# A half-size first gate/up product in the second block, wide score multiplications, and new engine orders

## The chip, the cores and the metric

The kernel runs on one core of one Trainium2 chip. The metric is the device time of one execution in microseconds (us); the time of a kernel is the median of several runs, and one further execution of it is recorded by the hardware profiler. The core has a matrix engine (TensorE; PE in the profile, with PEld for the loading of its weights), a vector engine (VectorE, DVE), an engine for activation functions and copies (ScalarE, ACT), a general engine (GpSimd, POOL) and an engine that only issues transfers here (SyncE, SP). Matrix products are accumulated in eight PSUM banks; everything else on the chip lies in SBUF.

## The reference

One sequence of 2048 tokens of width 1024 is normalised; the result goes through local attention and, beside it, through a gated feed-forward network, and both are joined:

```python
x = A_x
xn = _layernorm(x, axis=-1)
s = _A_ref(xn, A_wqkv, A_wo)           # 32 heads of 32; each token sees itself
...                                    # and the tokens 2, 4, ... 14 before it
g = _silu(_B_ref(xn, B_w1, B_w3, B_w2))  # (silu(xn w1) * (xn w3)) w2, hidden width 3584
return x + s * g
```

The scores of one token are eight products of its query with the keys at distances 0, 2, ..., 14 ("shifts" below), summed over 32 numbers of a head.

## The kernel before

**Tiling.** The tokens are worked in two blocks of 1024 (`b` = 0, 1), each of two chunks of 512 (`c` = 0, 1 and 2, 3). A block does the q, k and v products, the attention of its chunks, the gate and up products of the network in 14 steps (`up_step(b, fb)`, each of 256 hidden columns), and the down and output products.

**Products with fewer multiplications.** Nearly all matrix products are done by a scheme of seven half-size products in place of eight (sums of operand quarters are made on DVE beforehand, and sums of results afterwards on DVE and ACT). In a gate/up step the first of these seven products, `pa` with the weights `w1` and the first half of the normalised tokens, is itself either done plainly (two times four matmuls of 512 columns, named `mm ua` below) or once more by the scheme: `up_first(b, fb)` has seven products of two matmuls of 256 columns each, three copies on ACT (`ufork`, `us5p`, `usnap`) and one add on DVE (`ucc`). `L2F` says for which steps: 1 to 13 in both blocks. `up_first` needs quarter sums of the tokens, made by `x_sums2` (`xt1` to `xt4`), and of the weights, made in block 0 by `w_sums2` (`wss0`, `wss2`, `wss3`), kept in `s2_dram` and loaded in block 1 by the transfer `s2.fb` into the slot of `w1` and `w3`. The larger sums of the weights (`ws0` to `ws3`) go through `s_dram` and come back as `st.fb`.

**Scores.** `scores(c)` goes over the eight shifts `w`. For each it multiplies queries and shifted keys on DVE in two halves of 128x2048 (`qk`), adds the halves (`qa`), and, where two shifts have a pair of buffers, adds on for both shifts at once (`qb`, `qc`) into `E`. The buffers are the three places of the pool `att`.

**What sets the order.** All work is first listed as operations, numbered in the order in which the code makes them. A planner gives each engine a sequence by costs and due times. Then the table `ORDER` (one row each for PE, DVE, ACT, POOL and SP) moves operations: an entry (a, b) puts operation a right behind operation b on its engine. Every engine works strictly in its sequence, and SP and POOL issue transfers in theirs. A slot of the pool `r8` (six buffers of 1 MB) is filled anew only when the work on its old contents is done.

**The second block's start.** The output product `wo(1)` of block 0's second chunk ends while the gate/up steps of block 1 begin. It gathers its result in a slot `o1` of `r8`; products with the gate (`s_g`) and the input (`x_o`) are made on DVE in five pieces, and each piece is stored by a transfer `out` on SP's queue. The slot is then filled with `st.2`, the sums of step 2 of block 1. In the profile the helpers have one line each: L593 and L1283 are the matmuls (plain, and of `up_first`), L602 all two-operand DVE work, L607 ACT copies, L634 all transfers. The tile `a` is the pool `att`, `r` is `r8`, `k` is a pool of f32 halves, `mm` is PSUM.

Of the kernel before, what the change touches and what calls it, by code (L numbers as in the profile page):

```python
# [42 lines left out]
class Plan:  # L43
# [420 lines left out]
def kernel(  # L464
# [17 lines left out]
    CH = 512  # L482
# [7 lines left out]
    NJ = 8  # L490
    NR = 4
# [815 lines left out]
    def w_sums(fb):  # L1307
# [9 lines left out]
        if U2B and fb:  # L1317
            w_sums2(fb)
# [780 lines left out]
```

## Time and profile before

| what | value |
|---|---|
| median of 3 runs | 707.27 us (706.75 to 707.87) |
| the profiled execution's own time | 707.13 us |
| its span, first to last instruction | 705.4 us |
| busy on DVE | 676.4 us, 831 instructions |
| busy on ACT | 385.4 us, 752 instructions |
| busy on POOL | 40.6 us, 83 instructions |
| moved by DMA | 174.06 MB, mean 247 GB/s |

A group row of the profile gives line, engine, operation, output and inputs, shape and count, then busy time, the mean duration of one in ns, and the idle time before. Instructions of one engine overlap: a duration holds the pipeline's end too. So the price of one instruction in a row of them is read from start to start in the timeline, whose rows give start, length, engine and what was done, neighbours of one kind merged.

### The profile page before, as it was taken

To read this page: it belongs to the slowest core of one execution; us is meant where nothing else is said; L and a number is where in the kernel's file an instruction comes from. 1 tells how busy PE (TensorE), PEld (TensorE's weight loads), DVE (VectorE), ACT (ScalarE), POOL (GpSimd) and SP (SyncE) were. 2 spreads that over 40 slices of the span, in tenths; PEclk is the share of its full clock that TensorE was granted. 3 is DMA by queue.
4 is the path that set the end of the run, shared out by engine and by line. 5 is a ranking of instruction groups with operands and counts; after the bars stand their busy time and mean duration, and the time that the engine had idled before them with its cause. 6 is when DMAs were issued, how large, how long until landed. Compare 5 with 4: busy or idle time off the path is not lost.

```text
span 705.4 us, 9790 instructions
## 1 busy us (share of the span) xinstructions
PE 696.8 (99%) x3611; PEld 374.5 (53%) x3666; DVE 676.4 (96%) x831; ACT 385.4 (55%) x752; POOL 40.6 (6%) x83
## 2 busy tenths in 40 slices
PE   9999999999999999999999999999999999999997
PEld 5555555545545474744555554454555555656443
DVE  8889999999999999999979999999999999999877
ACT  6644465658465796812564454566756755222143
POOL 1001020012101000000010000000100010000000
PEclk9999999999999999999999999999999999999999
DMA  9998889787788899996776767976675668858403
GB/s 333 291 354 305 300 290 319 256 271 268 227 300 291 300 287 212 300 270 215 266 240 237 238 212 225 306 240 217 204 237 177 199 187 251 270 210 268 153 28 119
DMA packets 142351, 174.06 MB, mean 247 GB/s; under 512 B 16912, under 2 KB 117280, under 8 KB 135648
## 3 DMA queue, kind: packets, MB, share of 16 engines
q1 hardware_dynamic: 131408, 138.10, 62.0%
q0 software_dynamic: 6240, 33.84, 12.8%
q10 hardware_dynamic: 4656, 1.51, 1.0%
q8 instruction: 28, 0.46, 0.3%
q14 instruction: 19, 0.16, 0.1%
HBM read 117.31 MB, written 43.78 MB: 228 GB/s over the span
## 4 chain that ended last, share of the span: by engine, by line
PE 94%; DVE 3%; DMA 2%; issue 1%; SPq 0%; ACT 0%; DVEq 0%; ACTq 0%
PE mm L593 82%; PE mm L1554 6%; PE mm L1283 5%; DMA r<-s_dram 1%; DVE r L602 1%; DVE a L602 1%; DMA r<-in_A_x_dram 1%; DMA out_dram<-r 1%; PE mm L781 0%; DVE small L699 0%; SPq L634 0%; DVE r L715 0%; DVE xT L602 0%; DVE E L602 0%; ACT k L607 0%
## 5 line engine op out<-in xcount | busy, mean ns | idle before, releaser
L593 PEld LDWEIGHTS <-r 128*128 128x128 f16 (+1 forms) x2068 | 219.6, 108 | 192.0 <-DMA r<-in_A_wqkv_dram 0.5
L593 PE MATMUL mm<-xs,r 128*128 128x512 f16 x1280 | 305.2, 379 | 0.3 <-DMA r<-s_dram 0.2
L593 PE MATMUL mm<-xT,r 128*128 128x512 bf16 (+2 forms) x747 | 177.6, 369 | 2.1
L607 ACT COPY k<-mm 128x512 f32<-128x512 f32 (+1 forms) x226 | 121.0, 565 | 74.0 <-PE mm L593 54.0
L607 ACT COPY mm<-mm 128x512 f32<-128x512 f32 (+1 forms) x157 | 75.6, 487 | 117.0 <-DVE mm L602 36.1
L593 PE MATMUL mm<-r,h_sb 128*128 128x512 f16 (+1 forms) x581 | 130.1, 379 | 0.6
L593 PEld LDWEIGHTS <-h_sb 128*128 128x128 f16 (+1 forms) x680 | 66.6, 98 | 78.4
L602 DVE TENSOR_TENSOR a<-a 128x2048 bf16<-128x2048 bf16 (+7 forms) x106 | 106.7, 1011 | 0.3
L602 DVE TENSOR_TENSOR h_sb<-mm,k 128x1024 bf16<-128x1024 f32 x48 | 58.2, 1217 | 7.1 <-PE mm L593 3.9
L1283 PE MATMUL mm<-xT,r 128*128 128x256 f16 (+1 forms) x364 | 61.1, 273 | 0.0
L602 DVE TENSOR_TENSOR a<-qo,kT 128x2048 bf16<-128x2048 bf16 x48 | 57.5, 1218 | 0.3 <-ACT kT L607 0.2
L602 DVE TENSOR_TENSOR h_sb<-h_sb 128x1024 f16<-128x1024 bf16 (+7 forms) x74 | 55.0, 748 | 0.2
L1283 PEld LDWEIGHTS <-r 128*128 128x128 bf16 (+1 forms) x364 | 35.6, 98 | 32.0
L602 DVE TENSOR_TENSOR a<-E,vT 128x2048 bf16<-128x2048 bf16 x42 | 50.3, 1217 | 0.3 <-issue 0.3
L602 DVE TENSOR_TENSOR k<-mm,k 128x1024 f32<-128x1024 f32 (+1 forms) x44 | 44.8, 1023 | 2.2 <-PE mm L593 2.1
L624 ACT ACTIVATE k<-k 128x512 bf16<-128x512 f32 x56 | 34.7, 636 | 15.5 <-DVE k L602 15.4
L602 DVE TENSOR_TENSOR r<-r,r 128x1024 f16<-128x1024 f16 (+7 forms) x56 | 42.5, 768 | 0.1
L624 ACT ACTIVATE h_sb<-mm 128x512 bf16<-128x512 f32 x60 | 36.2, 611 | 5.7 <-PE mm L593 5.5
L602 DVE TENSOR_TENSOR qo<-qo,a 128x2048 bf16<-128x2048 bf16 x32 | 39.0, 1219 | 0.3
L602 DVE TENSOR_TENSOR r<-r 128x1024 f16<-128x1024 bf16 (+4 forms) x71 | 36.1, 515 | 0.2
L602 DVE TENSOR_TENSOR h_sb<-h_sb,k 128x2048 bf16<-128x2048 bf16 x28 | 34.1, 1218 | 1.3 <-ACT k L607 1.2
L607 ACT CAST k<-mm 128x512 bf16<-128x512 f32 x56 | 32.3, 598 | 0.9 <-PE mm L593 0.7
(129 smaller groups left out, 528.9 us busy)
## 6 DMA issues: line engine op xcount, KB each, us to landing
r<-in_B_w_dram SPq DMA_DIRECT2D x42, 512.0 KB, 5.4
s_dram<-r POOLq DMA_DIRECT2D x14, 1024.0 KB, 5.2
r<-s_dram SPq DMA_DIRECT2D x14, 1024.0 KB, 5.7
r<-t_dram SPq DMA_DIRECT2D x15, 896.0 KB, 6.8
r<-in_A_wqkv_dram SPq DMA_DIRECT2D x10, 1024.0 KB, 8.6
r<-in_B_w_dram SPq DMA_DIRECT2D x11, 896.0 KB, 5.6
h_sb<-in_B_w_dram SPq DMA_DIRECT2D x14, 512.0 KB, 6.8
t_dram<-h_sb POOLq DMA_DIRECT2D x7, 1024.0 KB, 6.3
```

What stands on the lines that cost most here:

```text
L593: nc.tensor.matmul(cut(ps.ap()), lhsT=lhs[k](), rhs=cut(rhs[k]()), start=(first and k == 0), stop=(last and k == n - 1), skip_group_check= ...
L602: plan.op(DVE, name, lambda: fn(out=o(), in0=a(), in1=b()), rd, wr, occ, 0.08, late=late)
L607: plan.op(ACT, name, lambda: nc.scalar.copy(out=o(), in_=a()), rd, wr, occ, 0.11)
L624: plan.op(ACT, name, lambda: nc.scalar.activation(out=o(), in_=a(), func=ACTF.Silu), rd, wr, occ, 0.11, table="silu")
L1283: nc.tensor.matmul(half(pa[i].ap, n)(), lhsT=A[0][k](), rhs=B[0][k](), start=first and k == 0, stop=k == 1, skip_group_check=True)
L1554: nc.tensor.matmul(half(bank.ap, n)(), lhsT=a[k](), rhs=c[k](), start=first and k == 0, stop=k == NQ - 1, skip_group_check=True)
```

## The change

Four edits in the code, and a new table `ORDER`:

- `L2F` has step 0 for block 1 too. `up_step(1, 0)` runs `up_first(1, 0)` whole ahead of its other products and leaves out the plain ones.
- For that, `w_sums(0)` makes the quarter sums of step 0 in block 0 and stores them, and `up_load(1, 0)` loads them (`s2.0`, 256 KB).
- For the shifts that have a pair of buffers (all eight of chunks 2 and 3, the first four of chunks 0 and 1: 24) `scores` does one multiplication of 128x4096 in place of two of 128x2048. The third buffer belongs to the pair for both shifts; the even shift's products lie in buffers 0 and 1, the odd one's in 1 and 2.
- Operation numbers shift with this, and the entries of `ORDER` are others: 281, 376, 321, 28 and 104 for the five engines, where 241, 396, 326, 23 and 104 stood.

```diff
-    L2F = {0: range(1, 14), 1: range(1, 14)}
+    L2F = {0: range(1, 14), 1: range(0, 14)}
...
                 if w % 2 == 0:
                     two = plan.pair("att", f"p{c}_{w}", f"p{c}_{w}")
+                    two.append(plan.slot("att", f"p{c}_{w}"))
             else:
                 two = None
-            for jh in range(2):
+            if two:
+                pr = two[w % 2:w % 2 + 2]
+                tt(f"qk{c}", mul, lambda w=w: plan.wide["att"][:, w % 2:w % 2 + 2].rearrange("p s (j n) -> p (s j) n", j=4),
+                   lambda: qo[:, u], lambda o=o: kv[:, :, o:o + CH],
+                   qo_cells(u, range(NJ)) + [x for j in range(NJ) for x in kc(j)] + ([x for j in range(NJ) for x in kh_(j)] if w else []),
+                   pr, 4096, True)
+            for jh in range(2) if not two else ():
...
-            if b in U2B and fb:
+            if b in U2B:
                 dma(SP, f"s2.{fb}", lambda: s2_v(wt).rearrange("p q k n -> p (q k n)"),
...
-        if U2B and fb:
+        if U2B:
             w_sums2(fb)
...
         more = up_first(b, fb + 1) if fb + 1 in L2F[b] else iter(())
+        if two and not fb:
+            for _ in up_first(b, fb):
+                pass
```

Of the new `ORDER`, the entries on SP that concern the second block's start, with the operations named (numbers of the new list):

```
(1766, 1687)  w3.0 behind xr             (1767, 1766)  s2.0 behind w3.0
(1794, 1727)  out 1794 behind out 1727   (1705, 1789)  out 1705 behind out 1789
(1720, 1705)  out 1720 behind out 1705   (1828, 1720)  s2.2 behind out 1720
```

Before, w3.0 stood behind the transfer `movev2`, further down the queue, s2.2 stood between the stores (behind the one that is 1720 now), and the stores 1789 and 1727 followed it.

More of the change, by code (lines that the diff above doesn't have):

```diff
@@ L1063, in scores @@
                 v = lambda two=two: two[0].both().rearrange("p w (j n) -> p w j n", j=4)
-                tt(f"qb{c}", add, lambda v=v: v()[:, :, 0:2], lambda v=v: v()[:, :, 0:2], lambda v=v: v()[:, :, 2:4], two, two, 2048, True)
+                tt(f"qb{c}", add, lambda v=v: v()[:, :, 0:2], lambda v=v: v()[:, :, 0:2], lambda v=v: v()[:, :, 2:4], two[0:2], two[0:2], 2048, True)
                 tt(f"qc{c}", add, lambda w=w: E[:, :, w - 1:w + 1, :].rearrange("p q w n -> p w q n"),
@@ L1067, in scores @@
                    lambda v=v: v()[:, :, 1].rearrange("p w (q n) -> p w q n", n=P),
-                   two, [("E", x, sq, r) for x in (w - 1, w) for sq in range(4) for r in range(NR)], 1024, True)
+                   two[0:2], [("E", x, sq, r) for x in (w - 1, w) for sq in range(4) for r in range(NR)], 1024, True)
                 if w % 4 == 3:
```

262 rows, old and new, of the table ORDER are left out of this document.

## The prediction

> **What bounds the kernel now.** I read the head of the page first, then a table of busy times by stretch, then the waits of PE alone, then PE's timeline at the one wait that is left.
>
> ```profile
> span 705.4 us, 9790 instructions
> ...
> PE 696.8 (99%) x3611; PEld 374.5 (53%) x3666; DVE 676.4 (96%) x831; ACT 385.4 (55%) x752; POOL 40.6 (6%) x83
> ```
>
> ```profile
> 0.00:21.00 21.00, 19.38 (x138) 12.75 (x140) 17.01 (x44) 14.40 (x32) 2.89 (x13) 1.00 1.01 312
> 21.00:421.00 400.00, 398.31 (x2008) 216.38 (x2041) 389.15 (x486) 231.96 (x441) 29.04 (x54) 1.00 0.83 272
> 421.00:452.00 31.00, 30.79 (x154) 15.06 (x154) 31.00 (x38) 15.78 (x33) 1.09 (x2) 1.00 0.82 248
> 452.00:694.00 242.00, 240.90 (x1277) 126.74 (x1296) 231.28 (x250) 121.24 (x244) 7.59 (x14) 1.00 0.63 203
> 694.00:705.40 11.40, 7.37 (x38) 3.54 (x37) 7.94 (x17) 2.03 (x5) 0.00 (x0) 1.00 0.48 158
> ```
>
> In the second fence each row gives a stretch, its length, the busy time (and count) of PE, PEld, DVE, ACT and POOL, the granted clock, the share of the DMA engines and GB/s. PE is the bound, and nearly without a hole: from 21 to 694 us it lacks 1.69 + 0.21 + 1.10 = 3.00 us of being busy. Most of that is not idle time: the page counts 3666 weight loads and only 3611 matmuls, so 55 matmuls have no record. DVE is nearly full too (31.00 of 31.00 us at the start of the second block), ACT is about half full, POOL nearly empty.
>
> ```profile
> PE mm L575 <- DVE k L573: 1.3, 1, 1.3
> PE mm L781 <- DVE r L715: 0.3, 1, 0.3
> PE mm L593 <- DMA r<-s_dram: 0.2, 1, 0.2
> ```
>
> The first two waits lie in the first 21 us. Only the third, for the transfer `r<-s_dram`, is in the body of the kernel. Here it is, with the price of matmuls around it:
>
> ```profile
> 450.05 0.60 PE L1283 MATMUL mm<-xT,r 128*128 128x256 bf16 x4
> 450.49 1.03 PE L593 MATMUL mm<-xs,r 128*128 128x512 f16 x4
> 451.35 0.60 PE L1283 MATMUL mm<-xT,r 128*128 128x256 f16 x4
> 452.15 3.63 PE L593 MATMUL mm<-xs,r 128*128 128x512 f16 x16 [0.20 <-DMA r<-s_dram]
> 455.62 0.38 PE L1283 MATMUL mm<-xT,r 128*128 128x256 f16 x2
> ```
>
> From start to start, four matmuls of 256 columns take 450.49 - 450.05 = 0.44 us, so 0.110 each, and sixteen of 512 columns 455.62 - 452.15 = 3.47 us, so 0.217 each (one lasts 3.63 - 15 x 0.217 = 0.38 us: a missing record leaves a hole of 2 x 0.217 - 0.38 = 0.054, and 55 of them are 3.0 us, the whole of what PE lacked). The half matmuls that began at 451.35 were through at 451.79; the next product began at 452.15. **PE lost 0.36 us there**, waiting for `st.2`. Why that transfer was late is in the chain of what ended last:
>
> ```profile
> 437.48 0.61 DVE r L602
> ...
> 438.11 0.38 SPq L634
> ...
> 439.54 3.61 DMA out_dram<-r
> ...
> 443.20 8.90 DMA r<-s_dram
> ```
>
> The third column is what ran. The last add on `o1` ended at 438.09, then the last three of its five stores had to be issued in turn (SP's queue, from 438.11 on); the last of them took 3.61 us, and only then, at 443.20, was the slot free for `st.2`, which took 8.90 us for its 1 MB.
>
> So the change can gain only where PE works less, or at that 0.36 us, or in the first 21 us (PE lacks 21.00 - 19.38 = 1.62) and after the last matmul (11.40 - 7.37 = 4.03). It can lose anywhere: there is no idle time on PE that would hide a new wait.
>
> **The half-size product on PE.** Step 0 of block 1 drops 8 matmuls of 512 columns, 8 x 0.217 = 1.74 us, and gets 14 of 256, 14 x 0.110 = 1.54. On the path: **-0.20 us**. The rest of the step stays.
>
> The Trainium skill, "TensorE: Matmul & The Clock Gate", section "Back-to-back issue gap", says the opposite for a real stream of weight load and matmul: about 81 ns for a matmul of 128 columns and 131 for one of 512. A third of the way in columns, that makes an estimate of 98 ns at 256, and 14 x 98 - 8 x 131 is 0.32 us more, not less. The rows above have 110 and 217 ns with a weight load at every matmul; here they decide.
>
> **What the new product needs.** Its seven parts are linked by three copies on ACT and the add `ucc` on DVE.
>
> ```profile
> 698.04 0.38 ACT L607 COPY mm<-mm 128x256 f32<-128x256 f32 x1
> ```
>
> ```profile
> 428.51 0.68 DVE L602 TENSOR_TENSOR r<-r,h_sb 128x1024 bf16<-128x1024 bf16 x1
> 429.11 1.22 DVE L602 TENSOR_TENSOR a<-a 128x2048 bf16<-128x2048 bf16 x1
> ...
> 441.40 0.69 DVE L602 TENSOR_TENSOR mm<-mm,k 128x512 f32<-128x512 f32 x1
> 442.00 0.68 DVE L602 TENSOR_TENSOR E<-a 128x1024 bf16<-128x1024 bf16 x1
> 442.60 3.49 DVE L602 TENSOR_TENSOR a<-qo,kT 128x2048 bf16<-128x2048 bf16 x3
> ```
>
> ```profile
> 420.46 1.89 PE L593 MATMUL mm<-r,qo 128*128 128x512 bf16 x7
> ...
> 428.23 1.89 PE L593 MATMUL mm<-xs,r 128*128 128x512 f16 x8
> ```
>
> A copy of 256 columns lasts 0.38 us, three 1.1 us; ACT has 31.00 - 15.78 = 15.2 us free in this stretch. `ucc` (the row `mm<-mm,k`) costs DVE 442.00 - 441.40 = 0.60 us, and it is a new wait: on the sixth part. The new PE row puts parts five and six behind `ue1_0`, which began at 428.23. It now begins 8 x 0.217 earlier and eight short matmuls (parts one to four) later, at 428.23 - 1.74 + 0.88 = 427.4; its four matmuls and four short ones end at 427.4 + 0.87 + 0.44, with the pipeline's end (0.38 - 0.22) at 428.9. On DVE `ucc` stands behind a `qa` (the row at 429.11) that moves ahead of the `s_g` of 428.51, so it starts one `qa` (1.14) after 428.5 less the savings: 429.5. Behind it wait an `s_g`, a wide multiplication and the remaining adds of `o1`. I take no wait, with 0.6 us to spare. Bounds: 0, and 0.9 us if the copies cost PE the whole lead of 1.74 - 0.88; all five pieces of `o1`, their stores and `st.2` would then be late by as much.
>
> **Weight sums of step 0.** Three more adds on DVE in block 0, of 512, 256 and 256 elements.
>
> ```profile
> 85.88 0.41 DVE L602 TENSOR_TENSOR r<-r 128x512 f16<-128x512 bf16 x1
> 86.22 1.21 DVE L602 TENSOR_TENSOR a<-a 128x2048 bf16<-128x2048 bf16 x1
> 87.35 0.28 DVE L602 TENSOR_TENSOR r<-r 128x256 f16<-128x256 bf16 x1
> 87.55 1.21 DVE L602 TENSOR_TENSOR a<-a 128x2048 bf16<-128x2048 bf16 x1
> ```
>
> They cost 86.22 - 85.88 = 0.34 and twice 87.55 - 87.35 = 0.20: 0.74 us, at about 85 us. POOL issues one store more, ahead of or behind others in a stretch of 400 us of which it is busy 29.04. The sums are read 330 us later.
>
> **Wide multiplications.** No row shows 128x4096. From start to start, 1024 elements take 442.60 - 442.00 = 0.60, and 2048 take (3.49 - 1.22) / 2 = 1.135 (the row x3 at 442.60). On that line 4096 take 1.135 + 2 x 0.535 = 2.20; without any gain they would take 2.27. I take 2.20, since the fixed part of the two rows, 0.07, is the same: 24 x 0.07 = 1.6 us less on DVE, bounds 0 and 1.6. With 0.74 + 0.60 added, DVE has between 0.3 us less and 1.3 us more to do, of 676.4; in the stretch from 21 to 421 us it has 400.00 - 389.15 = 10.9 us free, and PE does not wait for it. On the path: 0.
>
> **Transfers.** `s2.0` brings 256 KB more. In the new SP row, `w3.0` and `s2.0` stand right behind `xr`, ahead of `w1.0`, which so far went first; `putv3` and `st.0` follow.
>
> ```profile
> 412.89 0.38 SPq L634 DMA_DIRECT2D r<-in_B_w_dram  x1
> ```
>
> ```profile
> r<-s_dram SPq DMA_DIRECT2D x14, 1024.0 KB, 5.7
> ```
>
> `w1.0` was issued at 412.89, when its slot came free. Now it goes third, at the end of 1 MB: 412.9 + 2 x 0.4 + 5.7 (the median for 1 MB) is 419.4; by the slowest row above, 8.90, it is 422.6. The first part of the new product comes behind the two products of `wo(1)` in the row at 420.46 (seven matmuls recorded, eight done), at 420.46 + 8 x 0.217 = 422.2. I take 0; bounds 0 and 0.4 us. `w3.0` leaves the busy part of the queue, so the transfers from 428 on have 256 KB less ahead of them.
>
> **The 0.36 us.** `st.2` needs all five stores of `o1`. Before, the piece ended at 438.09 was stored first of the last three, with `s2.2` and two other stores issued behind it, the last at 439.54. Now that piece's store is last and `s2.2` behind it. Up to its add DVE does `ucc` more (0.60) and has four pairs fused (4 x 0.07): +0.3 us. So the last store goes out at 438.4, 1.1 us earlier; with the same 3.61 and 8.90 `st.2` lands at 451.0, against 451.6 at which PE asks for it (451.79 less the 0.20). **-0.36 us**, with 0.6 to spare. Bounds: -0.36, and +1.06 if the 256 KB of `s2.0` (at this stretch's 248 GB/s) still lie ahead of it in the queue and the stores gain nothing.
>
> **Sum.** -0.20 - 0.36 = -0.56 against the profiled execution: 707.13 - 0.56 = 706.57. The median was 0.14 above that execution, so 706.7 us, -0.08%. About 0.2%, 1.4 us, is what a measurement of this kernel can tell from no change: I forecast **no change that can be told**. The unknowns of the sum (+0.9, +0.4, and 1.4 at `st.2`) reach from 706.7 to 709.4.
>
> **Rivals.**
>
> *The wide multiplication holds up DVE (slower).* Sixteen of the 24 are interleaved with block 1's gate/up steps. An add on PSUM that becomes ready behind the start of a wide one waits up to 2.20 us, where it waited 1.135: up to 1.07 later. PE loses what exceeds the slack of the bank that the add frees.
>
> ```profile
> ACT mm L607 <- DVE mm L602: 36.1, 19, 3.9
> ```
>
> For it: copies into PSUM wait for DVE's adds as it is, 19 times, 36.1 us in all, and DVE has no idle time in that stretch to catch up. Against it: not one wait of PE for DVE after the first 21 us. It decides the sign once four of the sixteen cost PE 0.5 each, given the 0.56 gained. With eight at 0.4: 706.7 + 3.2 = 709.9.
>
> *The queue.* `st.2` comes later by the 1.06 us of `s2.0`, and its wait becomes 1.42: 707.27 - 0.20 + 1.06 = 708.1. For it: the DMA engines are 0.82 busy there. Against it: `w3.0`, as large, is taken out of that part.
>
> *The change does not reach the wait.* `st.2` stays as late as it was, and only the 0.20 shows: 707.07.
>
> *Clearly faster.* That needs 1.4 us: the 0.56, and 0.9 of the 1.62 that PE lacks in the first 21 us. There PE waits on the arrival of the input and on the first sums, which no edit touches; only the orders could: 705.7.
>
> **How the numbers follow.** Chances: the forecast 0.52, DVE held up 0.18, the queue 0.15, no reach 0.08, clearly faster 0.07. The Trainium skill's rule (+0.32 in place of -0.20, so 707.2) gets under 0.01, inside the last but one. The queue's case lies on the bound of 1.4 us, so half of it counts as slower: slower 0.18 + 0.08 = 0.26, faster 0.07, the rest 0.67. The range goes from 705.7, at the edge of the faster case, to 709.8, where half of DVE's case and the queue's upper bound lie inside; it leaves out 0.05 below and 0.10 above.
>
> **What will show it.** Right: 378 matmuls of 256 columns in the group of `up_first` where 364 stood; 24 products of 128x4096 that take 2.20 us from start to start; `w1.0` landed before 422; the last store of `o1` issued near 438.4, `st.2` issued before 442.5, and no wait of PE for `r<-s_dram`. Wrong: any row in which PE waits for DVE or ACT after 21 us, above all in 421 to 590 us; a wide product at more than 2.27; a wait of PE ahead of the first half matmuls of block 1; `ucc` on DVE after an idle gap.

## The result, and the profile after

The changed kernel takes 709.56 us (median of 6 runs, 709.08 to 711.13); the kernel before took 707.13 us on the same chip (6 runs, 706.75 to 707.87). The ratio of the means is 1.0039, with an interval of 1.0026 to 1.0052: **0.39% slower**; the medians are 2.4 us apart. The prediction was 706.7 us with "no change that can be told" as the likeliest case. The time lies inside the range (705.7 to 709.8), but the forecast of no change that can be told was wrong.

The head of the page after:

```profile
span 707.5 us, 9802 instructions
...
PE 697.0 (99%) x3617; PEld 374.7 (53%) x3672; DVE 676.5 (96%) x811; ACT 387.8 (55%) x755; POOL 41.2 (6%) x84
```

PE is as busy as before to 0.2 us, and the span is 2.1 us longer: nearly all of the added time is idle time of PE. The profiled execution took 709.34 us, 2.21 more than that of before. The table of stretches (its columns are those of the prediction) says where:

```profile
21.00:421.00 400.00, 396.46 (x1999) 214.96 (x2030) 387.10 (x477) 230.13 (x435) 29.61 (x55) 1.00 0.82 269
421.00:452.00 31.00, 30.69 (x158) 15.42 (x160) 30.49 (x34) 18.02 (x38) 1.10 (x2) 1.00 0.95 297
452.00:694.00 242.00, 241.05 (x1283) 127.05 (x1299) 231.83 (x240) 121.81 (x244) 7.58 (x14) 1.00 0.63 202
```

The second block, where most of the edits work, is as it was to 0.15 us (30.79 and 240.90 us before). From 21 to 421 us PE is busy 396.46 us where it was 398.31: 1.85 less. Cut finer, all of that lies in one stretch of block 0, where the prediction had put nothing on the path. Before, then after:

```profile
52.00:110.00 58.00, 57.74 (x278) 31.73 (x282) 57.41 (x73) 29.74 (x57) 5.83 (x11) 1.00 0.85 300
```

```profile
52.00:110.00 58.00, 55.88 (x266) 30.35 (x270) 54.44 (x63) 28.28 (x53) 4.78 (x9) 1.00 0.84 294
```

The waits of PE after:

```profile
PE mm L595 <- DVE r L604: 1.3, 1, 1.3
PE mm L577 <- DVE k L575: 1.2, 1, 1.2
PE mm L783 <- DVE r L717: 0.6, 2, 0.3
PE mm L595 <- DVE h_sb L604: 0.4, 1, 0.4
PE mm L595 <- ACT mm L609: 0.2, 1, 0.2
PE mm L595 <- DMA r<-s_dram: 0.2, 1, 0.2
```

The second and third lie in the first 21 us. They are those of before with one of 0.3 us added, which leaves nothing behind: the first row of PE past 24 us starts at 24.37 before and at 24.38 after. The other four are new (the last one is not the wait for `st.2`). Here they are in PE's timeline:

```profile
57.19 1.03 PE L595 MATMUL mm<-xT,r 128*128 128x512 bf16 x3
59.47 2.78 PE L595 MATMUL mm<-xs,r 128*128 128x512 f16 x12 [1.25 <-DVE r L604]
...
84.78 1.67 PE L595 MATMUL mm<-xs,r 128*128 128x512 f16 x7
86.83 1.89 PE L595 MATMUL mm<-xs,r 128*128 128x512 f16 x8 [0.38 <-DVE h_sb L604]
...
96.77 3.76 PE L595 MATMUL mm<-xs,r 128*128 128x512 f16 x16
100.37 0.38 PE L1292 MATMUL mm<-xT,r 128*128 128x256 f16 x2
100.97 1.02 PE L595 MATMUL mm<-xT,r 128*128 128x512 bf16 x4 [0.23 <-ACT mm L609]
...
429.94 0.38 PE L1292 MATMUL mm<-xT,r 128*128 128x256 bf16 x2
430.47 1.04 PE L595 MATMUL mm<-xs,r 128*128 128x512 f16 x4 [0.15 <-DMA r<-s_dram]
```

With 0.217 us for a matmul of 512 columns and 0.110 for one of 256, the loss is read from start to start. Four products from 57.19 (three have a record) end at 58.06, the next starts at 59.47: 1.41. Seven from 84.78 end at 86.30, next 86.83: 0.53. Sixteen from 96.77 end at 100.24, next 100.37: 0.13; two short ones end at 100.59, next 100.97: 0.38. Two short ones from 429.94 end at 430.16, next 430.47: 0.31. Together 2.76 lost. Less the 0.20 and 0.36 that the prediction counted as gained, that is **+2.20, against 2.21 measured**. The agreement to 0.01 is chance: PE's last row starts at 702.71 where it started at 700.38, so 2.32 later if counted from the row past 24 us, and what follows it is about 0.1 shorter. To 0.1 us the balance holds. So the whole question is where these five holes come from.

The largest is a wait for `r`, here the sum `qs0`, the first sum of the v weights. The chain of what ended last passes through it (start, length, what ran):

```profile
41.44 16.65 DMA r<-in_A_wqkv_dram
...
58.18 1.23 DVE r L604
```

The second half of the v weights (1 MB) took 16.65 us to come, and the sum waited for it. DVE before, then DVE after, around that sum (`r<-r,r` of 128x2048):

```profile
55.66 1.22 DVE L602 TENSOR_TENSOR h_sb<-mm,k 128x1024 bf16<-128x1024 f32 x1
56.80 1.21 DVE L602 TENSOR_TENSOR r<-r,r 128x2048 f16<-128x2048 bf16 x1
58.24 1.22 DVE L602 TENSOR_TENSOR h_sb<-mm,k 128x1024 bf16<-128x1024 f32 x1 [0.23 <-PE mm L593]
```

```profile
54.00 1.23 DVE L604 TENSOR_TENSOR h_sb<-mm,k 128x1024 bf16<-128x1024 f32 x1 [0.43 <-PE mm L595]
58.18 1.23 DVE L604 TENSOR_TENSOR r<-r,r 128x2048 f16<-128x2048 bf16 x1 [2.96 <-DMA r<-in_A_wqkv_dram]
59.33 0.68 DVE L604 TENSOR_TENSOR h_sb<-h_sb 128x1024 f16<-128x1024 bf16 x1
59.93 1.22 DVE L604 TENSOR_TENSOR h_sb<-mm,k 128x1024 bf16<-128x1024 f32 x1
```

In the new sequence the sum stands right behind the piece of 54.00, and DVE waits 2.96 us in front of it, with two instructions (59.33 and 59.93) behind it that were ready: e11 below runs them at 55.13 and 56.51. That is nearly all of what DVE lacks in the stretch (58.00 - 54.44 = 3.56). Before, DVE ran 57.41 of 58.00 us there.

### The profile page after: what moved, and what is told of

It is laid out like the page before. It is cut to its first block, busy times and chain, and to the rows that moved or that the text cites. A ratio compares the mean times of both kernels' runs of the same rounds, so it can differ in the third digit from the quotient of the medians.

```text
span 707.5 us, 9802 instructions
## 1 busy us (share of the span) xinstructions
PE 697.0 (99%) x3617; PEld 374.7 (53%) x3672; DVE 676.5 (96%) x811; ACT 387.8 (55%) x755; POOL 41.2 (6%) x84
## 3 DMA queue, kind: packets, MB, share of 16 engines
q10 hardware_dynamic: 4656, 1.51, 1.3%
## 4 chain that ended last, share of the span: by engine, by line
PE 86%; DVE 8%; DMA 4%; issue 1%; ACT 0%; SPq 0%; DVEq 0%
PE mm L595 74%; PE mm L1566 6%; PE mm L1292 5%; DMA r<-in_A_wqkv_dram 2%; DVE r L604 2%; DVE a L604 2%; DVE h_sb L604 2%; DMA r<-s_dram 1%; DVE xT L604 1%; DMA r<-in_A_x_dram 1%; PE mm L783 0%; DVE small L701 0%; DVE k L604 0%; DVE r L717 0%; ACT r L609 0%
## 5 line engine op out<-in xcount | busy, mean ns | idle before, releaser
L595 PEld LDWEIGHTS <-r 128*128 128x128 f16 (+1 forms) x2060 | 218.6, 108 | 193.5 <-DVE r L604 2.2
L595 PEld LDWEIGHTS <-h_sb 128*128 128x128 f16 (+1 forms) x680 | 66.5, 98 | 77.8
L1292 PE MATMUL mm<-xT,r 128*128 128x256 f16 (+1 forms) x378 | 63.2, 273 | 0.0
L604 DVE TENSOR_TENSOR a<-qo,kT 128x4096 bf16<-128x4096 bf16 (+1 forms) x32 | 56.0, 1760 | 0.3
L604 DVE TENSOR_TENSOR h_sb<-h_sb 128x1024 f16<-128x1024 bf16 (+7 forms) x74 | 55.2, 755 | 0.1
L1292 PEld LDWEIGHTS <-r 128*128 128x128 f16 (+1 forms) x378 | 37.0, 98 | 32.9
L604 DVE TENSOR_TENSOR r<-r 128x1024 f16<-128x1024 bf16 (+3 forms) x74 | 37.7, 516 | 0.7 <-PE mm L595 0.5
```

Source lines behind the costliest of these rows:

```text
L595: nc.tensor.matmul(cut(ps.ap()), lhsT=lhs[k](), rhs=cut(rhs[k]()), start=(first and k == 0), stop=(last and k == n - 1), skip_group_check= ...
L604: plan.op(DVE, name, lambda: fn(out=o(), in0=a(), in1=b()), rd, wr, occ, 0.08, late=late)
L1292: nc.tensor.matmul(half(pa[i].ap, n)(), lhsT=A[0][k](), rhs=B[0][k](), start=first and k == 0, stop=k == 1, skip_group_check=True)
```

## The experiments

Edits of sequences are shown as the names of the operations in an engine's sequence, with their numbers in the list of the kernel that was changed. `w2s` is a sum of the down product's weights, stored by `t_dram`; `put_sq1_0` and `put_sq1_1` store sums of the k weights (1 MB each, like `t_dram`, all on POOL's queue); `qev`, `qbk` are v and k products on PE; `qc12`, `qc22`, `uh`, `ua2`, `ucc` are sums of results on DVE. The table holds all runs: the median time, the ratio of the means to the kernel before run beside it, with its interval, when the second half of the v weights landed, and what PE lost from start to start, worked out as above from the one execution that was profiled. The 0.36 us of the kernel before at 452 us lie in none of its columns.

| run | us | ratio | landed | lost at 46 to 70 us | at 84 to 87 | at 88 to 101 | at 430 |
|---|---|---|---|---|---|---|---|
| before | 707.13 | | 56.42 | 0 | 0 | 0 | 0 |
| after | 709.56 | 1.0039 [1.0026, 1.0052] | 58.09 | 1.41 | 0.53 | 0.51 | 0.31 |
| e1_sum_later | 709.38 | 1.0033 [1.0021, 1.0046] | 58.20 | 1.62 | 0.53 | 0.54 | 0.60 |
| e2_narrow | 709.57 | 1.0033 [1.0021, 1.0045] | 58.58 | 1.43 | 0.54 | 0.58 | 0 |
| e3_plain | 710.93 | 1.0054 [1.0037, 1.007] | 57.99 | 1.24 | 0 | 0.45 | 0 |
| e4_before_sum_earlier | 707.54 | 1.0004 [0.9995, 1.0013] | 57.03 | 0 | 0 | 0 | 0 |
| e5_store_first | 709.87 | 1.0037 [1.0024, 1.0049] | 58.46 | 1.51 | 0.54 | 0.54 | 0 |
| e6_before_store_held | 707.75 | 1.0006 [0.9997, 1.0015] | 57.51 | 0.56 | 0 | 0 | 0 |
| e7_store_first_putv | 710.01 | 1.0042 [1.0028, 1.0057] | 58.60 | 1.73 | 0.54 | 0.54 | 0 |
| e8_both_moves | 707.96 | 1.0012 [1.0003, 1.002] | 56.13 | 0.37 | 0 | 0.54 | 0 |
| e10_before_with_sums | 707.79 | 1.0008 [0.9999, 1.0017] | 57.26 | 0 | 0 | 0.62 | 0 |
| e11_sums_wait | 707.95 | 1.0011 [1.0002, 1.0021] | 57.97 | 0 | 0.47 | 0.54 | 0 |
| e13_before_st2 | 707.17 | 1.0000 [0.9991, 1.0009] | 56.63 | 0 | 0 | 0 | 0 |
| e14_new_orders | 713.57 | 1.0097 [1.0084, 1.011] | 57.83 | 5.52 | 0 | 0 | 0 |
| e15_new_orders_store | 708.18 | 1.0026 [1.0011, 1.0041] | 58.72 | 2.90 | 0 | 0 | 0.21 |
| e16_orders_late_load | 711.71 | 1.0063 [1.0049, 1.0077] | 58.23 | 5.14 | 0 | 0 | 0 |
| e17_orders_store | 709.67 | 1.0028 [1.0017, 1.004] | 57.98 | 1.61 | 0 | 0.19 | 0.36 |
| e18_sums_wait_late | 707.13 | 0.9995 [0.9986, 1.0004] | 58.51 | 0 | 0 | 0 | 0 |

**Is it an edit of the code?** Two runs kept the new sequences and took one edit each out of the code.

```diff
-            if two:
...
-            for jh in range(2) if not two else ():
+            for jh in range(2):
```

> The changed kernel's sequences with each wide multiplication as two of 128x2048 again, one right behind the other. Transfer theory: the load is as late as in the changed kernel, all its waits stay, and DVE has 24 x 0.07 us more to do: 709.6 to 710.2. Rival (the wide multiplication holds up DVE's adds): 2 us or more faster, 707.5 or less.

```diff
-    L2F = {0: range(1, 14), 1: range(0, 14)}
+    L2F = {0: range(1, 14), 1: range(1, 14)}
```

> The changed kernel's sequences without the half-size step: no quarter sums of step 0 (0.74 us less on DVE at 80 us), no s2.0, the plain first products of step 0 in block 1 where parts three and four stood. Transfer theory: the wait of 1.42 at 57.8 us stays; those at 86 to 100 us shrink by up to 0.74; PE does 0.20 more, and up to 1 us may be lost in block 1, where the sequences do not fit the plain products: 709.2 to 710.8. Rival (the half-size step is what costs): 707.5 or less.

Without the wide multiplications the time is 709.57, the same as with them. Without the half-size step and its weight sums the hole at 58 us stays (1.24), the one at 86 us goes, and new ones come in 445 to 456 us, where the plain products no longer fit the sequence; its time (its runs reach from 709.16 to 713.97) says nothing on its own. So no edit of the code makes the hole at 58 us: the sequences do.

**Why the load is late.** It was issued at the same time as before (41.4). In the new order the store of the weight sums (`t_dram`) is issued ahead of `put_sq1_0`, and a second one at 49.85 and not at 55.70. One run put the sum that releases the second store behind `qs0`, one swapped the first two stores, one did both; two runs put like moves into the kernel before, the other way round.

```diff
 DVE:  xt4 358, w2s 169
-      w2s 164
       qc22 268, qc12 265, qc12 285, qs0 289
+      w2s 164
```

> The changed kernel with one addition moved on DVE: the last of the four sums that release the second store to t_dram stands behind the first sum of the v weights (qs0) instead of ahead of it, so that 1 MB store cannot start before the second half of the v weights has landed. Transfer theory (the early store takes the bandwidth from that load, DVE waits 2.96 us for it and PE 1.42 at 57.8 us, and the waits of PE at 86, 98 and 100 us, 1.1 together, come from the same lateness of DVE): the load lands 1.5 to 3 us earlier, all four waits go, 709.6 - 2.5 = 707.1. Rival (the edits load DVE too much in block 0): the wait at 57.8 may shrink, those at 86 to 100 stay, 708.1 or more.

```diff
 POOL:
+      put_sq1_0 245
       t_dram 158
-      put_sq1_0 245
       put_sq1_1 246
```

> The changed kernel with one pair exchanged on POOL: put_sq1_0, whose data are done at 36.6 us, is issued ahead of the first store to t_dram, behind which it waited until 42.0. Queue-head theory (POOL's first entry holds up 1 MB while the DMA engines are half idle, so everything behind it, the second half of the v weights too, lands 2 to 3 us later): put_sq1_0 issued near 37, the v weights landed by 56, no wait of PE at 57.8, those at 86 to 100 us smaller by half or more; 709.4 - 1.4 - 0.5 to 1.1 = 706.9 to 707.5. Rival (the edits load DVE too much): the load lands as late as now or PE waits as long elsewhere in 52 to 110 us: 708.5 or more.

With both of these edits:

> The kernel after, with the first 1 MB store of GpSimd's queue set ahead of the store of the weight sums (as in the run with the store first) and, on VectorE, the weight sum that releases the second store of weight sums set behind the first sum of the v weights (as in the run with the sum later). Each alone left the last half of the v weights landing near 58.3 us. Theory of the transfers (the load ends when GpSimd's later stores of 1 MB end): both together let it land near 56 us, TensorE's wait of 1.4 us at 58 us goes to 0.3 or less, and the time is 708.1 if the waits at 86, 98 and 100 us stay, 707.2 if they were its consequence. Rival (the new sequences simply ask for the sums of the v weights earlier than any such load can land): load still near 58 us and 709.5.

In the kernel before, first the sum alone, then the two stores swapped with another sum moved back:

```diff
 DVE:  w2s 163
+      w2s 164
       qc12 265, w2s 169, w2s 170
-      w2s 164
```

> The kernel before, with the same addition moved the other way: up two places on DVE, into the idle time at 47.7 us, so that the second store to t_dram starts about 7 us earlier; nothing else differs. Transfer theory: the second half of the v weights lands 1.5 to 2 us later than 56.4 us, DVE waits for it, and PE waits 1 to 2.5 us in 57 to 100 us: 708.1 to 709.6. Rival (the edits are the cause, the order of the store is harmless): 707.1.

```diff
 POOL:
+      t_dram 158
       put_sq1_0 245
-      t_dram 158
 DVE:
-      w2s 157
       qc22a 238
+      w2s 157
```

> The kernel before, with the changed kernel's order put into it at that place alone: on POOL the first store to t_dram stands ahead of put_sq1_0, and the sum that releases it comes five places later on DVE, at about 41.7 us. Queue-head theory: the v weights land at 58 or later where it was 56.4, DVE waits for them, PE loses 1 to 2.5 us between 50 and 100 us: 708.1 to 709.6. Rival (the edits cost, not this order): 707.1 to 707.4.

Either move alone changed nothing (58.20 and 58.46); my theory of one store failed twice. Both together brought the load 2 us earlier and with it the time to 707.96. The time to landing of both halves, least, median and most, in the kernel after and in that run (the second half was issued at 41.44 and at 41.72):

```profile
DMA to landing us min/median/max: 6.5/11.6/16.6
```

```profile
DMA to landing us min/median/max: 12.2/13.3/14.4
```

The first half came later and the second earlier: moving the two stores shifted both halves. In the kernel before, the same kind of move delayed the load to 57.03 and 57.51 and cost nothing that the times can tell, though the trace of e6 has holes of 0.33 and 0.21 us. At these landings the old sequences lose little, the new ones 1.4 us at 58.1, so the place of the sum is to be tried by itself.

**The place of the sum.** Nothing of the transfers is touched here. On VectorE one sum of results and two weight sums go ahead of `qs0`, on TensorE two k products ahead of the two v products that need it.

```diff
 DVE:  qc12 285
-      qs0 289
       w2s 170, qc22 288, w2s 171
+      qs0 289
 PE:   qav1 296
-      qev1 298, qev0 297
       qbk2 299, qbk3 301
+      qev1 298, qev0 297
```

> The kernel after, with nothing of its transfers changed: on VectorE the first sum of the v weights goes behind one group of 2.4 us of score-half multiplications' kind and two weight sums (1.23 + 0.68 + 0.68 us) that the trace shows waiting behind it, and on TensorE the two products that need it go behind two others of 0.87 us each. Theory of the slack (the sum stands too early in the new sequences; VectorE idles 2.96 us in front of it, and this time is what it lacks at 86, 98 and 100 us): the load still lands near 58.1 us, VectorE idles under 0.6 us there, TensorE's wait of 1.4 us goes to 0.2 or less, those at 86, 98 and 100 us (1.1 us together) go down to 0.3 or less in all, and the time is 707.0 to 707.5. Theory that the three new weight sums of step 0 fill VectorE in any case: the wait at 58 us goes, those at 86 to 100 us stay or grow, 708.1. If neither: 709.5.

DVE in that run:

```profile
55.13 0.68 DVE L589 TENSOR_TENSOR h_sb<-h_sb 128x1024 f16<-128x1024 bf16 x1
56.51 1.22 DVE L589 TENSOR_TENSOR h_sb<-mm,k 128x1024 bf16<-128x1024 f32 x1 [0.70 <-PE mm L580]
57.65 0.68 DVE L589 TENSOR_TENSOR h_sb<-h_sb 128x1024 f16<-128x1024 bf16 x1
58.25 2.48 DVE L589 TENSOR_TENSOR r<-r,r 128x2048 f16<-128x2048 bf16 x2
```

The load lands as late as in the kernel after (57.97), the sum starts as late (58.25), and PE loses nothing there: 707.95 us. An earlier load (e8) and a later demand (e11) are worth the same, 1.6 us by the medians (ratios of 1.0012 and 1.0011, where the kernel after has 1.0039). The wait at 86 us falls only to 0.47, and those at 97 to 100 us stay at 0.54 in both runs: the first half of my expectation held (the hole at 58), the second did not.

**The weight sums of step 0.** What is left could be their price. In the kernel before, alone:

```diff
-        if U2B and fb:
+        if U2B:
             w_sums2(fb)
...
 DVE:  ws3 353
+      wss0, wss2, wss3
```

> The kernel before, with the three quarter sums of the weights of step 0 and their store added in the first block and read by nothing: the cost of the new weight sums by themselves, which the prediction put at nothing. VectorE gets 0.74 us more near 85 us. If VectorE has room there: 707.1 to 707.2. If its sequence is full from there to 100 us, TensorE waits up to 0.7 us for a gate product's input near 97 us: 707.5 to 707.8.

The time is 0.58 us above the kernel before (interval -0.1 to +1.2); the time alone does not tell it from nothing, but the trace shows the hole that was expected, 0.62 us at 96.8 (the rows below: four products from 96.15 end at 97.02, the next starts at 97.64):

```profile
96.15 1.03 PE L581 MATMUL mm<-xs,r 128*128 128x512 f16 x4
97.64 1.02 PE L581 MATMUL mm<-xs,r 128*128 128x512 f16 x4 [0.46 <-DVE h_sb L590]
```

So 0.74 us more on a DVE without room cost 0.6, in this order. Whether an order exists in which they cost nothing was tried with five new ones. Four of them cover 45 to 112 us; the edits below are those that proved to matter.

> The kernel after, code and transfers as they are, with the sequences of TensorE, VectorE and ScalarE between 45 and 112 us ordered anew (62 instructions or groups moved by a few places) so that the first sum of the v weights may come as late as 58 us and no score multiplication or weight sum stands ahead of a sum that TensorE waits for at 85 to 100 us. All three weight sums of step 0, the wide multiplications and the half-size step are kept. Theory of the order (all that the change loses is lost by where these sums stand, none by the added work itself): the waits at 58, 86, 98 and 100 us (2.5 us together) go to 0.3 or less, the half-size step and the store ahead of st.2 show their gain, less what st.0 takes at 430 us: 706.5 to 706.9, so below the kernel before. Theory of the added work (VectorE is full between 60 and 100 us and the 1.0 us of new weight sums must show): 707.6 to 707.9, as in the two runs with one move each.

```diff
 DVE:
-      qs0 289, w2s 170, qc22 288
+      qs0 289, qs1 290, w2s 170, qc22 288
```

> The same kind of new order on top of the kernel with both moves (GpSimd's store of 1 MB first, the weight sum behind the first sum of the v weights), whose load landed at 56.1 us. Theory of the order: as in the other run, 706.5 to 706.9. If an earlier landing were worth something by itself, this one is the faster of the two by up to 0.4 us.

> The kernel after, code and transfers as they are (all weight sums of step 0, the wide multiplications and the half-size step kept), with a new order of TensorE, VectorE and ScalarE between 45 and 112 us, chosen so that no product of TensorE needs the first sum of the v weights before about 60 us and nothing that TensorE needs stands on VectorE behind that sum. The last new order failed in this: a sum of 1.2 us that TensorE needed at 58 us stood behind it. Theory of the order (what the change loses is lost by where these instructions stand): load still near 58 us, the waits at 58, 86, 98 and 100 us (2.5 us together) go to 0.3 or less, 706.5 to 706.9. Theory of the added work (VectorE full from 60 to 100 us): 707.6 to 707.9 as in the runs with one move.

```diff
 DVE:
-      qs0 289, w2s 170, qc22 288, w2s 171, qs1 290, w2s 175
+      qs2 292, qc22 288, w2s 175, w2s 176, w2s 177, qs0 289, qs1 290
```

> A second order of the same kind, on the kernel with GpSimd's 1 MB store first and the weight sum behind the first sum of the v weights, where the load landed at 56.1 us. Theory of the order: 706.5 to 706.9, the same as the other within 0.3 us, since the landing no longer matters; theory of the transfers (an earlier landing is worth something by itself): this one faster by 0.3 us or more.

All four lost near 60 us. In the first (and the second), `qc22`, which PE needed at 58 us, stood behind the late `qs0`, and PE waited:

```profile
62.20 2.29 PE L580 MATMUL mm<-xs,r 128*128 128x512 f16 x5 [3.78 <-DVE h_sb L589]
```

In the third, three sums that wait for another load, landed at 62.11, stood ahead of `qs0` (in the fourth, two). DVE in the third:

```profile
62.14 2.15 DVE L589 TENSOR_TENSOR h_sb<-h_sb 128x1024 f16<-128x1024 bf16 x3 [3.04 <-DMA h_sb<-in_B_w_dram]
64.20 2.48 DVE L589 TENSOR_TENSOR r<-r,r 128x2048 f16<-128x2048 bf16 x2
```

They say nothing on the weight sums, but they show how dear the wrong place is: one instruction on DVE waiting for a transfer holds up all behind it.

In the first and the third the hole is not the whole loss. In the first PE stood still from 58.28 to 62.20, 3.92 us, and then 16 matmuls took 5.07 us, up to 67.27, where 16 x 0.217 is 3.47: 1.60 more (the losses of the table hold this part too). The clock that was granted to PE (the third figure from the end) is about half there, and 1.00 in the stretches before and after:

```profile
62.00:65.50 3.50, 3.31 (x8) 1.28 (x8) 3.50 (x5) 0.59 (x1) 0.00 (x0) 0.51 0.74 184
```

In the third it is 0.51 from 66.5 to 70.0 us, behind a hole of 2.87 us. In the second, a hole of 2.90 us left it at 1.00, in the execution that was profiled. So a long hole may be paid for again, and not each time.

The second and the fourth were meant to have both moves of e8. They have the swapped stores alone: the sum `w2s` 164 stands ahead of `qs0` again, the second store went out at 51.03 and 50.62 us, and the load landed at 58.72 and 57.98. So they don't show what an earlier landing is worth. The second had runs from 706.94 to 711.96 us; what makes them differ is open.

The fifth kept e11 up to 60 us on DVE and up to 76 us on PE and ACT, and ordered only what follows, with all landings as in e11's trace; for instance `uh`, the sum that PE needs at 97 us (`ws1` and `ws3` move further up, out of this cut):

```diff
 DVE:
-      qb 1039, ws0 415, ws1 366, ws2 417, ws3 368, qc 1040, w2s 189, uh 410, ucc 409, ua2 401
+      ws0 415, qb 1039, uh 410, w2s 189, ua2 401, ws2 417, qc 1040, ucc 409
```

> The kernel with the first sum of the v weights moved back (707.95 us, waits of TensorE left at 84.6, 96.7 and 98.9 us, 0.9 us together), unchanged up to 60 us on VectorE and up to 76 us on TensorE and ScalarE, and ordered anew from there to 112 us with the landings of all loads as its trace shows them. All added weight sums are kept. Theory of the order: these three waits go to 0.2 or less in all and the time is 706.9 to 707.2, no slower than before. Theory of the added work (VectorE is full there, whatever the order): the waits stay between 0.6 and 0.9 us, 707.6 to 708.0. The two new orders that failed put sums that TensorE needed at 58 to 62 us behind another late load; here that stretch is left as it is.

`uh` in e11, and then in this run:

```profile
95.81 1.22 DVE L589 TENSOR_TENSOR h_sb<-mm,k 128x1024 bf16<-128x1024 f32 x1
```

```profile
93.22 1.22 DVE L589 TENSOR_TENSOR h_sb<-mm,k 128x1024 bf16<-128x1024 f32 x1
```

And PE in this run, as a table of stretches and in its waits:

```profile
52.00:110.00 58.00, 57.73 (x278) 31.63 (x282) 56.89 (x66) 28.75 (x55) 5.30 (x10) 1.00 0.83 294
```

```profile
PE mm L562 <- DVE k L560: 1.3, 1, 1.3
PE mm L580 <- DMA r<-in_A_wqkv_dram: 1.1, 2, 0.9
```

Both waits lie in the first 15 us; from there on PE loses nothing, though the load lands at 58.51, later than in any of the good runs. 707.13 us, against 707.59 for the kernel before beside it (0.9995 [0.9986, 1.0004]). The code is that of the changed kernel, all weight sums and wide multiplications included: **the 2.4 us lie in the order, from 45 to 112 us**, as far as these runs can tell. By its times it is not shown to be faster than the kernel before. The traces say more: from the first row of 32 matmuls to PE's last row, the kernel before takes 700.38 - 27.82 = 672.56 us and this run 700.41 - 28.40 = 672.01, so 0.55 less, where the prediction counted 0.56. This execution only reached that first row 0.58 us later. Before, then this run:

```profile
27.82 7.07 PE L593 MATMUL mm<-xs,r 128*128 128x512 f16 x32
...
700.38 1.04 PE L618 MATMUL mm<-h_sb,qo 128*128 128x256 f16 x8
```

```profile
28.40 7.07 PE L580 MATMUL mm<-xs,r 128*128 128x512 f16 x32
...
700.41 1.04 PE L605 MATMUL mm<-h_sb,qo 128*128 128x256 f16 x8
```

**The store ahead of `st.2`, alone.** In the kernel before, `s2.2` goes behind the last store of `o1`.

```diff
 SP:
-      s2.2 1830
       out 1791, out 1731
+      s2.2 1830
       w1.2 1827, st.2 1828
```

> The kernel before, with one issue of SyncE's queue moved: the load s2.2 goes behind the last output store of the attention (o1), so that this store and with it the load st.2, which waits for it, are issued 0.5 us earlier. The prediction counted 0.36 us for TensorE's wait at 451.8 us going in this way: 706.75 if it is so and nothing else moves (st.2 lands near 451.6 in place of 452.1). If the load st.2 is held by the other transfers and not by its issue: 707.1.

PE there, where it lost 0.36 us before (four short products from 451.56 end at 452.00, the next starts at 451.99):

```profile
451.56 0.60 PE L1271 MATMUL mm<-xT,r 128*128 128x256 f16 x4
451.99 3.19 PE L581 MATMUL mm<-xs,r 128*128 128x512 f16 x14
```

The wait is gone: `st.2` was issued at 441.97 and not at 443.20. From the row of 32 matmuls to the last row this run takes 700.21 - 28.02 = 672.19 us, 0.37 less than before; its time, 707.17 against 707.21, cannot tell that from nothing. But e4, e6 and e10, in which this queue is as before, show no wait there either (in e4 `st.2` was issued at 443.58, landed at 451.71, and PE came to it 0.3 us later than in the kernel before). So the move makes the load earlier, as was expected, but the 0.36 us are not a loss of every execution.

**The wait at 430 us.** `st.0` was issued at 421.49 and landed at 430.42, 0.31 late. The run below set the 1 MB store `putv3` behind `s2.1`, on top of the swapped stores of POOL:

```diff
 SP:
-      putv3
       w1.1, s2.1
+      putv3
```

> As e5_store_first, and on SP the store putv3 of 1 MB comes behind w1.1 and s2.1 instead of right behind st.0, with which it shared the engines while PE waited 0.31 us for st.0 at 430 us. If that sharing made st.0 late: st.0 lands 1.5 us earlier or more, the wait at 430 goes, 0.3 us less than e5_store_first: 706.6 to 707.2, below the kernel before by the 0.2 to 0.56 of the prediction. If not: as e5_store_first.

`st.0` took 5.98 us there, 7.94 in the run without that move (e5) and 8.94 after. So `putv3` does hold it up by 2 us, but e5 has no wait either, and the time (710.01, e5 709.87) shows no gain: PE waits only where the load takes nearly 9 us, and what makes the last 1 us is open.

## Why the prediction was wrong

**The half-size product, -0.20: as worked out.** 378 matmuls stand in the group of `up_first`, as said:

```profile
L1292 PE MATMUL mm<-xT,r 128*128 128x256 f16 (+1 forms) x378 | 63.2, 273 | 0.0
```

Neither e13 nor e18 has a hole in PE's rows between the row of 32 matmuls and the last one. They take 672.19 and 672.01 us, and e18 has the half-size product: 0.18 less. That is one execution of each, and below what the times can tell.

**The wide multiplication, 2.20 each: right.** 421.85 - 419.64 = 2.21 us:

```profile
419.64 2.29 DVE L604 TENSOR_TENSOR a<-qo,kT 128x4096 bf16<-128x4096 bf16 x1
421.85 0.68 DVE L604 TENSOR_TENSOR h_sb<-qo,h_sb 128x1024 f16<-128x1024 bf16 x1
```

The rival that a wide one holds up DVE did not come about: PE does not wait for DVE once after 110 us, and e2 without them takes the same time. The sign named for it, a row in which PE waits for DVE or ACT after 21 us, did come, but at 58 to 101 us and not in the second block. That this rival's 709.9 lies near the result is chance; the place and the mechanism are others.

**The 0.36 us at `st.2`: right, for what that wait is worth.** All five stores are issued ahead of the next load, and PE's rows follow each other without a hole (451.87 + 4 x 0.110 = 452.31). The times named, 438.4 for the last store and "before 442.5" for `st.2`, were 440.90 and 444.59: the 2.5 us that block 0 had lost came on top. In e18, which did not lose them, they are 438.93 and 442.39. As said beside e13, the wait was no fixed loss to begin with.

```profile
438.56 2.72 SPq L636 DMA_DIRECT2D out_dram<-r  x5
```

```profile
451.87 0.60 PE L1292 MATMUL mm<-xT,r 128*128 128x256 bf16 x4
452.31 1.89 PE L595 MATMUL mm<-xs,r 128*128 128x512 f16 x8
```

**`ucc` and the transfers: right in sign.** `ucc` starts on DVE without an idle gap. The bound of 0.4 us for the transfers holds the 0.31 at `st.0`, which is one queue entry further than the transfer I had looked at. That transfer, `w1.0`, landed at 423.4, not before 422, for the same reason (in e18 at 421.2); PE, which needed it at 424.75, did not wait for it.

**The weight sums of step 0, 0.74 us on DVE, "On the path: 0": failed.** The room was read from 21 to 421 us, where DVE has 10.9 us free. At 52 to 110 us, where the sums stand, it has 58.00 - 57.41 = 0.59. e10's trace shows 0.6 us for them in the old order, e18's none in a good one.

**The new entries of `ORDER` in the first block: the step that was missing.** I read the order only on SP and only around the second block's start; the first 100 us got no term, on the ground that of DVE's work there "PE does not wait for it". That is a statement about the old sequences, and it was these that changed. "Clearly faster" even says that "only the orders could" move the start of the kernel; the same sentence with the other sign is what happened. The missing term is 2.45 us: 1.41 for `qs0` in front of a load that lands at 58.1, and 0.53, 0.13 and 0.38 where sums that PE needs stand behind weight sums and score work that could wait. I first took these last three for a consequence of the first (what DVE idles at 58 it lacks later); e8 and e11 remove the first and keep 0.54 and 1.01 of the others, so for the most part they are holes of their own.

What would have shown it: each instruction that the new sequence on DVE moves ahead of a late load, against the time at which that load lands in the trace of before. `qs0` started at 56.80 there, and the load had landed only at 56.42: 0.38 us of slack, in the old order. The new one asks for the sum behind the piece that ends at 55.2.

## What to carry to other kernels

A new order is a change of its own, in every stretch that it touches: check each instruction that waits for a transfer against the landing that the trace shows, not against the time at which it was planned to land. Where an engine is full, put what waits for a transfer behind all ready work that others need; here one sum in the wrong place was worth 1.4 us, and three more 1 us together; in the run with the worst order, a hole of 3.9 us cost 1.6 us more at half the clock. And read the room for added work from a stretch as short as the work's own neighbourhood: 10.9 us free in 400 was 0.6 us where it counted.

## What the runs showed of the hardware

The same load, the second half of the v weights, issued within 0.7 us of the same time on SP's queue (41.36 to 42.01), landed between 56.1 and 58.7 us, with the stores of POOL's queue around it at different times. The order of two stores and the release of a third moved it by 2 us only together (58.46 and 58.20 for one alone, 56.13 for both). In the kernel after it was issued at 41.44 and landed at 58.09, while a 1 MB store issued at 44.12 on the other queue landed at 57.46.

The Trainium skill, "DMA: Bandwidth & Descriptors", section "Queues, rings and completion order", says that each DMA engine takes turns between its queues packet by packet. By that rule an earlier transfer of one queue need not land ahead of a later one of another. The two landings above agree with it, but no run isolates the turns themselves.

The clock granted to TensorE fell to half for about 3.4 us behind idle times of 3.9 us (e14) and 2.9 us (e16), and a matmul of 512 columns then took 0.43 us from start to start where it takes 0.217. Another idle time of 2.9 us (e15) was not followed by it; what decides is not shown.
